# Attention and a gated feed-forward on one core: the order of all queues searched anew, with a port lock in the plan and products on zeros at the start

## The chip, the cores and the metric

One core of a Trainium2 chip runs the whole program in one launch. The metric is device microseconds of one execution; below, TensorE is called PE, VectorE DVE, ScalarE ACT, GpSimd POOL, and SyncE, which issues every DMA, SP, as in the profile.

## The reference

Inputs q, k, v are (8 batches, 8 heads, 576 positions, 64), float32. Everything downstream of `attn_out` is a token-shifted feed-forward with a squared ReLU and a sigmoid gate.

```python
# attention: a coarse one on means of 4 positions, plus a local one (|i - j| < 4)
q_d, k_d, v_d = (x.reshape(B, H, S // 4, 4, D).mean(axis=3) for x in (q, k, v))
out_up = np.repeat(softmax(q_d @ k_d.T / 8) @ v_d, 4, axis=2)
out_local = softmax(where(|i - j| < 4, q @ k.T / 8, -1e9)) @ v
x = (out_up + out_local).transpose(0, 2, 1, 3).reshape(B, S, 512)
# feed-forward
x_prev = x shifted by one position (zeros first)
xk = mu_k * x + (1 - mu_k) * x_prev ;  xr = mu_r * x + (1 - mu_r) * x_prev
out = sigmoid(xr @ w_r) * (maximum(xk @ w_k, 0) ** 2 @ w_v)
```

The weights w_k (512 x 1024), w_v (1024 x 512) and w_r (512 x 512) arrive as 64-bit floats.

## The kernel before

**Tiling.** The attention goes by 32 steps n = 0..31, each a pair of heads of one batch (four steps make a batch). A step turns q and k (`flip` on PE and `turn_part` for the first five, a DVE transpose after that), sums them by fours (`pool_q`, `pool_k`, `pool_v`), makes the scores on PE (`score_both`, later `run_pe`, which also holds the value products of the step before), and goes through two softmaxes: the coarse one (`down_top`, `down_exp`, `down_sum`, `down_norm`, `down_turn`, `down_copy`) and the local one (`score_top`, `score_sub`, `score_exp`, `score_sum`, `score_norm`, `score_turn`, `spread`). `av_pe` multiplies with v; `av_up`, `av_two`, `av_out` put the sum into the tile `xt` of the batch. All scores of a step lie in one PSUM tile, of which there is one.

The feed-forward goes by ten chunks c of 512 or 256 positions. The mix of a chunk is `mix_prev` (x_prev scaled), `mix_part` (mu times x added), `mix_high` and `mix_low`, the two halves into which a float32 is split for products in the faster number format. For chunk 0 the mix xk is made on PE instead (`mix_pe` with diagonal matrices, then `mix_split`, `mix_rest`). Then come eight `k_pe` (12 products of 512 columns each), `k_relu`, `k_high` (square and high half), `k_low`, the gates (`r_pe`, `gate`), 16 `v_pe`, `store_mul` and `store_out`.

Each of the 20 weight blocks of 512 KB is fetched and turned from 64-bit to two halves: `weight_scale` (ACT), `weight_shift` and `weight_tail` (DVE), `weight_high` (ACT), and the low half by `weight_diff` on PE with `weight_left` on ACT (blocks 0 to 7, those of w_k) or by `weight_low` on POOL.

**Order.** The class `Plan` holds every step as a task with its engine, its time and its tiles. `arrange` goes through the tasks in the order that the string `ORDER` spells (two characters a task), gives each a start by its model, chooses PSUM banks, and the program is emitted in that order; so each engine's queue is fixed by the string, and every engine works its queue in order. `fill` then puts products on the matrix `nidn` (`keep_warm`, line 482) where the model sees PE idle in the first 100 us. An SP task in those 100 us also waits until the DMAs before it, but for the last 5.2 us of modelled transfer, have landed (`landed_before`, line 1268).

## Time and profile before

| | us |
|---|---|
| runs | 645.09 median of 3 (644.08, 645.09, 646.65) |
| span of the profiled execution, first to last instruction | 644.7 |
| PE busy | 628.7 (98%) |
| DVE, ACT, POOL busy | 423.2 (66%), 426.4 (66%), 310.4 (48%) |
| DMA, mean over the span | 112 GB/s |
| first `k_pe` begins at | 68.24 |
| last run of products (12 of L972) | 637.55 to 640.46 |

The span is the profiled execution's own time; no other figure for that execution is given, and it lies 0.4 us under the median. Matmuls overlap their neighbours, so a busy PE need not be one at its best; the stretch before the first `k_pe`, called the prologue here, is where PE works in many small steps.

### The profile page before, as it was taken

To read this page: it belongs to the slowest core of one execution; us is meant where nothing else is said; L and a number is where in the kernel's file an instruction comes from. 1 tells how busy PE (TensorE), PEld (TensorE's weight loads), DVE (VectorE), ACT (ScalarE), POOL (GpSimd) and SP (SyncE) were. 2 spreads that over 40 slices of the span, in tenths; PEclk is the share of its full clock that TensorE was granted. 3 is DMA by queue.
4 is the path that set the end of the run, shared out by engine and by line. 5 is a ranking of instruction groups with operands and counts; after the bars stand their busy time and mean duration, and the time that the engine had idled before them with its cause. 6 is when DMAs were issued, how large, how long until landed. Compare 5 with 4: busy or idle time off the path is not lost.

```text
span 644.7 us, 17973 instructions
## 1 busy us (share of the span) xinstructions
PE 628.7 (98%) x6984; PEld 517.5 (80%) x6984; DVE 423.2 (66%) x796; ACT 426.4 (66%) x993; POOL 310.4 (48%) x465
## 2 busy tenths in 40 slices
PE   6989999999999999999999999999999999999997
PEld 6666788878888887888888888888888788888886
DVE  3885966598578876874489856697578744612312
ACT  4886966666767857784859775677667847634442
POOL 5686799855762657334454546345763440000000
PEclk9997999999999999999999999999999999999999
DMA  8888987635566464615655546546574320100001
GB/s 266 282 228 164 230 134 132 132 63 121 116 142 120 107 135 86 137 29 121 138 130 119 107 95 125 101 92 137 111 147 104 86 59 0 50 17 0 25 11 65
DMA packets 251574, 71.90 MB, mean 112 GB/s; under 512 B 224346, under 2 KB 243170, under 8 KB 251490
## 3 DMA queue, kind: packets, MB, share of 16 engines
q1 hardware_dynamic: 251490, 70.76, 49.6%
q8 instruction: 55, 0.90, 0.6%
q14 instruction: 29, 0.24, 0.1%
HBM read 56.85 MB, written 13.86 MB: 110 GB/s over the span
## 4 chain that ended last, share of the span: by engine, by line
PE 83%; DMA 5%; DVE 5%; POOL 2%; SPq 2%; ACT 1%; issue 1%; DVEq 0%; POOLq 0%; ACTq 0%
PE ps_g L940 29%; PE acc L988 28%; PE ps_r L972 12%; PE ps_v L796 6%; PE ps_a L646 3%; DMA wk<-in_moe_w_k_dram 2%; DVE mix L910 2%; DMA kraw<-in_k_dram 2%; PE ps_a L709 1%; PE ps_m L918 1%; PE ps_f L552 1%; DMA wv<-in_moe_w_v_dram 1%; PE ps_a L651 1%; DVE xks L932 1%; DMA qraw<-in_q_dram 1%
## 5 line engine op out<-in xcount | busy, mean ns | idle before, releaser
L940 PE MATMUL ps_g<-xks,wk 128*128 128x512 f32 (+1 forms) x960 | 207.0, 370 | 1.8 <-DVE xks L932 1.0
L940 PEld LDWEIGHTS ps_g<-xks,wk 128*128 128x128 f32 x960 | 168.0, 189 | 33.9 <-DVE xks L932 1.3
L988 PE MATMUL acc<-wv,kh 128*128 128x512 f32 x578 | 180.4, 393 | 0.0
L988 PEld LDWEIGHTS acc<-wv,kh 128*128 128x128 f32 x578 | 106.3, 188 | 22.1
L988 PE MATMUL acc<-wv,kl 128*128 128x512 f32 x289 | 112.6, 390 | 0.0
L972 PE MATMUL ps_r<-wr,xr 128*128 128x512 f32 x432 | 104.0, 392 | 0.1
L972 PEld LDWEIGHTS ps_r<-wr,xr 128*128 128x128 f32 x432 | 80.5, 188 | 17.5 <-DVE xr L932 0.5
L910 DVE SCALAR_TENSOR_TENSOR mix<-xt,mus,mix 128x256 f32<-128x256 f32 (+3 forms) x184 | 88.5, 527 | 7.6 <-ACT mix L905 7.4
L960 DVE TENSOR_TENSOR kl<-kk,kh 128x512 fp32r<-128x512 f32 (+1 forms) x63 | 45.5, 723 | 68.2 <-ACT kh L953 68.0
L742 POOL TENSOR_TENSOR an<-ad,sd 64x144 f32<-64x144 f32 (+2 forms) x128 | 66.7, 531 | 31.9 <-DVE sd L733 24.6
L947 ACT ACTIVATE kk<-ps_g 128x512 f32<-128x512 f32 (+1 forms) x80 | 43.3, 548 | 55.6 <-PE ps_g L940 51.6
L905 ACT ACTIVATE mix<-xt,mus 128x256 f32<-128x256 f32 (+3 forms) x184 | 71.1, 441 | 3.6 <-DVE xr L932 2.2
L674 POOL TENSOR_TENSOR sm<-sm,mx 128x384 f32<-128x384 f32 x28 | 23.9, 853 | 96.5 <-DVE mx L669 96.4
L960 POOL TENSOR_TENSOR kl<-kk,kh 128x512 fp32r<-128x512 f32 (+1 forms) x17 | 21.2, 1251 | 92.7 <-ACT kh L953 52.5
L988 PEld LDWEIGHTS acc<-wv,kl 128*128 128x128 f32 x289 | 54.3, 188 | 11.8 <-DVE kl L960 0.4
L953 ACT ACTIVATE kh<-kk 128x512 fp32r<-128x512 f32 (+1 forms) x80 | 47.2, 589 | 17.1 <-PE acc L988 15.0
L796 PE MATMUL ps_v<-bd,vw 64*64 64x48 f32 x1536 | 52.2, 219 | 1.1 <-issue 1.1
L796 PEld LDWEIGHTS ps_v<-bd,vw 64*64 64x64 f32 x1536 | 48.0, 136 | 1.3 <-issue 1.3
L610 POOL TENSOR_TENSOR tk<-kz 64x288 f32<-64x288 f32 (+1 forms) x56 | 39.8, 711 | 18.6 <-DVE kz L590 7.4
L952 ACT ACTIVATE kk<-kk 128x512 f32<-128x512 f32 (+1 forms) x80 | 46.5, 581 | 0.8
L688 POOL TENSOR_TENSOR sm<-sm,ssum 128x384 f32<-128x384 f32 x32 | 29.2, 913 | 28.8 <-DVE ssum L684 17.1
L864 ACT ACTIVATE up<-ps_v 128x144 f32<-128x144 f32 x32 | 9.3, 290 | 50.0 <-PE ps_v L796 25.7
(108 smaller groups left out, 984.3 us busy)
## 6 DMA issues: line engine op xcount, KB each, us to landing
vw<-in_v_dram SPq DMA_DIRECT2D x126, 96.0 KB, 2.9
out_dram<-sig SPq DMA_DIRECT2D x35, 256.0 KB, 2.3
v<-in_v_dram SPq DMA_DIRECT2D x32, 256.0 KB, 3.6
qraw<-in_q_dram SPq DMA_DIRECT2D x108, 72.0 KB, 2.5
kraw<-in_k_dram SPq DMA_DIRECT2D x108, 72.0 KB, 2.5
wk<-in_moe_w_k_dram SPq DMA_DIRECT2D x8, 512.0 KB, 5.7
wv<-in_moe_w_v_dram SPq DMA_DIRECT2D x8, 512.0 KB, 6.2
keys<-blocks SPq DMA_DIRECT2D x96, 40.0 KB, 1.8
```

Source lines behind the costliest of these rows:

```text
L610: nc.gpsimd.tensor_tensor(out=tk[h], in0=k4[:, :, 0:2], in1=k4[:, :, 2:4], op=ALU.add)
L742: nc.gpsimd.tensor_tensor(out=x, in0=y, in1=z, op=ALU.mult)
L796: nc.tensor.matmul(pv[r][64 * e:64 * e + 64, cols], lhs, rhs, start=(i == 1), stop=(i == NG + 1 + (r != e)))
L905: nc.scalar.activation(mixes[c, h, nm][:, p, o:o + L], xts[b][:, p, s:s + L], AF.Copy, scale=rest)
L910: nc.vector.scalar_tensor_tensor(out=to[:, p, o:o + L], in0=xts[b][:, p, s + 1:s + 1 + L], scalar=mu[:, p:p + 1], in1=to[:, p, o:o + L], o ...
L940: nc.tensor.matmul(ps, w_k_part(p, f, w), x[:, :, y, p, :], start=(m == 0), stop=(m == len(mm) - 1))
L947: nc.scalar.activation(kk, kq[c, f].rearrange("p h t -> p (h t)"), AF.Relu)
L952: nc.scalar.activation(kk, kk, AF.Square)
L953: nc.scalar.activation(kh, kk, AF.Copy)
L960: eng.tensor_tensor(out=kl, in0=kk, in1=kh.bitcast(F32), op=ALU.subtract)
L972: nc.tensor.matmul(ps, x[:, y, p, o:o + P], ws[f"r{p}"][:, w, :], start=(m == 0), stop=(m == len(mm) - 1))
L988: nc.tensor.matmul(accs[c, t][:, j], x[:, o:o + P], ws[f"v{f}"][:, w, j], start=(f == 0 and m == 0), stop=(f == NF - 1 and m == 2), skip_g ...
```

## The change

It replaces the model in `Plan.arrange`, the string `ORDER`, and the engine of 239 of the 1992 tasks, and changes a few steps at the start:

- The model takes DVE and POOL as holders of one exclusive port lock for the operations in `LOCKED` (each part of an operation waits until the other engine's part has ended), and a clock for PE that depends on its recent work.
- A string table `ELSE` moves tasks to another engine. Read out, it moves, from ACT to DVE: 57 `mix_prev`, 19 `mix_high`, 13 `av_up`, 9 `spread`, 5 `weight_high`, 3 `down_copy`; from POOL to DVE: 20 `score_norm`, 13 `pool_k`, 9 `pool_q`, 9 `pool_v`, 9 `score_sub`, 9 `k_low`, 3 `down_norm`, 1 `weight_low`; from POOL to ACT: 22 `down_norm`; from DVE to POOL: 27 `k_low`; and 11 `turn_part` change between ACT and DVE.
- `fill` and its `keep_warm` products go (`FILLERS = ()`). In their place `clear_warm` (DVE) clears 128 columns, and `warm` lets PE multiply them nine times, before the first `flip`.
- `load_consts` is split into `load_identity` and `load_band`; the first DMA is now q of step 0.
- `clear_edge` clears the edge of a window of v on POOL, in tasks of their own, not on DVE inside `load_windows`.
- The diagonals use the buffer of `xr`, not one of the two of `f32tmp`.
- Steps named in `HEADS`, `BITS`, `WPSUM`, `MIXPS` exist in the code, but those lists are empty, so nothing of them is emitted.

The strings read out, from the start to the last window of v that the prologue needs (SP), and to the first `k_pe` (PE; wd is `weight_diff`, sb `score_both`, dt `down_turn`; the 37 steps are the same ones, and `warm` is new). w is a fetch of a weight block, q and k a `load_raw`, v4 and win the two loads of v:

```
SP before  consts q0 k0 w4 q1 w3 w1 k1 q2 w0 w2 w10 mus k2 w5 v4.0 q3 w8 w13 k3 q4 w7 v4.1 w19 k4
           win0 w6 w16 v4.2 win1 w11 win2 v4.3 win3
SP after   q0 ident k0 q1 w1 band w3 w5 k1 q2 w0 mus w7 k2 w4 w13 v4.1 q3 k3 v4.0 w2 q4 w6 k4
           w8 win0 w10 win1 win2 v4.3 v4.2 win3
PE before  flip0q flip0k flip1q sb0 flip1k flip2q wd3 sb1 mus flip2k wd1 wd4 flip3q wd0 wd2 dt0 sb2 wd5
           flip3k wd7 flip4k flip4q av0 dt1 sb3 mix0 wd6 av1 dt2 sb4 av2 dt3 mix1 av3 mix2 mix3 dt4 k_pe
PE after   warm flip0q flip0k sb0 flip1q wd1 flip1k wd3 flip2q flip2k sb1 wd5 wd4 wd0 mus flip3q sb2 dt0
           flip3k wd7 flip4k flip4q wd2 sb3 av0 dt1 wd6 av1 dt2 sb4 mix0 av2 dt3 mix1 av3 mix2 dt4 mix3 k_pe
```

Before the first `k_pe`, the queue of DVE holds `weight_shift` and `weight_tail` for 14 blocks before the change and for 11 after it.

```diff
-KLPOOL, KLF = 1, (3,)
-FLIPACT = (("q", 1), ("k", 0))
+HEADS = ()
+FILLERS = ()
+WARM = 9
 ORDER = """
...
+ELSE = dict(
+    ACT="""
...
-    SHARED = "weight_low k_low mix_low mix_part pool_v".split()
+    LOCKED = dict(
+        DVE=("weight_low k_low mix_low mix_part mix0_low mix0_part pool_v pool_q pool_k score_sub score_norm down_norm "
+             "weight_high mix_high mix0_high mix_prev mix0_prev spread weight_bits").split(),
+        POOL="weight_low k_low pool_v pool_q pool_k score_sub score_norm down_norm diagonals double_mask weight_bits".split())
...
+        def part_of(eng, now, us):
+            got, others = now + self.ENTER, pair[other[eng]]
+            while any(x <= got < y for x, y in others):
+                got = next(y for x, y in others if x <= got < y)
+            e = got - self.ENTER + us
...
+    def clear_warm():
+        nc.vector.memset(xks[:, 0, 0, 0, 0:P].bitcast(F32), 0.0)
+
+    def warm(bank):
+        ps = pp.tile([P, 512], F32, tag=plan.bank[bank], name="ps_x", bufs=1)
+        x = xks[:, 0, 0, 0, 0:P]
+        for _ in range(WARM):
+            nc.tensor.matmul(ps.rearrange("p (a c) -> p a c", a=4), x, x[:, None, :].broadcast_to([P, 4, P]), start=True, stop=True)
+
+    def clear_edge(n):
+        st.setdefault(n, {})["vw"] = vw = wp.tile([P, 12, D], F32, tag="vw", name="vw", bufs=3)
+        if n == 0:
+            nc.gpsimd.memset(vw[0:32, 0, :], 0.0)
+        else:
+            nc.gpsimd.memset(vw[96:128, 11, :], 0.0)
...
+    def engine():
+        return {"DVE": nc.vector, "POOL": nc.gpsimd}[now["eng"]]
+
+    def copied(out, x, **scale):
+        if now["eng"] == "ACT":
+            nc.scalar.activation(out, x, AF.Copy, **scale)
+        elif scale:
+            nc.vector.tensor_scalar(out=out, in0=x, scalar1=scale["scale"], scalar2=None, op0=ALU.mult)
+        else:
+            engine().tensor_copy(out=out, in_=x)
...
-            nc.scalar.activation(mixes[c, h, nm][:, p, o:o + L], xts[b][:, p, s:s + L], AF.Copy, scale=rest)
+            copied(mixes[c, h, nm][:, p, o:o + L], xts[b][:, p, s:s + L], scale=rest)
...
-        nc.scalar.activation(mixed(c, h, nm)[:, 0], mixes[c, h, nm], AF.Copy)
+        copied(mixed(c, h, nm)[:, 0], mixes[c, h, nm])
...
-    emitted = plan.fill(plan.arrange(), keep_warm)
...
+    for t in plan.arrange():
+        now["eng"] = t["eng"]
```

## Rows read from the trace of the kernel before

**Rows 1.** The page: instructions' busy time by engine over the span.

```profile
PE 628.7 (98%) x6984; PEld 517.5 (80%) x6984; DVE 423.2 (66%) x796; ACT 426.4 (66%) x993; POOL 310.4 (48%) x465
```

**Rows 2.** Busy time by stretch; last three columns: granted clock, DMA share, GB/s.

```profile
5.86:11.23 5.37, 5.37 (x101) 5.37 (x102) 1.58 (x3) 2.66 (x5) 2.07 (x10) 1.00 0.98 367
11.23:36.10 24.87, 23.97 (x564) 17.53 (x561) 20.93 (x41) 20.01 (x50) 15.56 (x27) 1.00 0.87 279
36.10:55.60 19.50, 16.54 (x501) 13.39 (x501) 15.06 (x33) 15.09 (x43) 17.07 (x28) 1.00 0.89 202
55.60:62.40 6.80, 6.80 (x52) 4.26 (x55) 2.83 (x7) 3.80 (x14) 3.83 (x7) 0.50 0.77 143
62.40:68.24 5.84, 5.72 (x53) 3.23 (x47) 4.38 (x10) 4.75 (x12) 3.05 (x5) 1.00 1.21 230
68.24:560.00 491.76, 489.86 (x5332) 405.45 (x5333) 355.95 (x668) 343.10 (x800) 261.42 (x378) 1.00 0.52 108
560.00:640.44 80.44, 80.44 (x403) 68.27 (x401) 21.74 (x37) 34.82 (x69) 2.03 (x2) 1.00 0.07 26
```

**Rows 3.** Timeline of the first 38 us, SP and PE: start, us, engine, line, what.

```profile
0.73 0.68 SPq L389 DMA_DIRECT2D mask<-in_band_dram  x1
...
5.86 2.19 PE L552 MATMUL ps_f<-small,qraw 64*64 64x64 f32 x36 [5.86 <-DMA qraw<-in_q_dram]
...
9.73 1.92 PE L552 MATMUL ps_f<-small,qraw 64*64 64x64 f32 x36
...
13.92 1.26 PE L552 MATMUL ps_f<-idn,kraw 64*64 64x64 f32 x36
...
37.29 1.27 PE L552 MATMUL ps_f<-idn,kraw 64*64 64x64 f32 x36 [1.16 <-DMA kraw<-in_k_dram]
```

**Rows 4.** Timeline of PE between 45 and 71 us.

```profile
45.20 1.99 PE L918 MATMUL ps_m<-xt,diag 128*128 128x512 f32 x4
...
54.37 0.29 PE L796 MATMUL ps_v<-bd,vw 64*64 64x48 f32 x4 [1.07 <-issue]
...
57.41 3.76 PE L918 MATMUL ps_m<-xt,diag 128*128 128x512 f32 x4
...
68.24 3.01 PE L940 MATMUL ps_g<-xks,wk 128*128 128x512 f32 x12
```

**Rows 5.** The chain that ended last, in order of time: start, us, what.

```profile
2.13 3.59 DMA qraw<-in_q_dram
...
10.37 6.09 DMA wk<-in_moe_w_k_dram
...
32.44 4.72 DMA kraw<-in_k_dram
...
67.49 0.70 DVE xks L925
```

**Rows 6.** Waits of PE over the span: who for whom, total, times, longest.

```profile
PE ps_g L940 <- DVE xks L932: 1.0, 1, 1.0
```

**Rows 7.** Timeline of DVE and of POOL from 70.5 us.

```profile
70.95 2.67 DVE L910 SCALAR_TENSOR_TENSOR mix<-xt,mus,mix 128x256 f32<-128x256 f32 x3
...
71.84 1.50 POOL L491 TENSOR_TENSOR wr<-w,wr 128x512 fp32r<-128x512 f32 x1 [0.31 <-ACT wr L469]
```

**Rows 8.** Groups of DVE and of POOL by form: busy, mean ns, idle before.

```profile
L910 DVE SCALAR_TENSOR_TENSOR mix<-xt,mus,mix 128x256 f32<-128x256 f32 x88 | 51.7, 612 | 6.1 <-ACT mix L905 6.0
L960 DVE TENSOR_TENSOR kl<-kk,kh 128x512 fp32r<-128x512 f32 x49 | 37.9, 776 | 53.6 <-ACT kh L953 53.4
...
L932 DVE TENSOR_TENSOR xks<-mix,xks 128x1024 fp32r<-128x1024 f32 x16 | 20.4, 1275 | 9.8 <-ACT xks L928 9.8
...
L668 DVE TENSOR_TENSOR sm<-ps_a,mask 128x384 f32<-128x384 f32 x28 | 15.3, 548 | 7.9 <-PE ps_a L709 6.9 <-ACT ad L726 0.9
...
L610 POOL TENSOR_TENSOR tk<-kz 64x288 f32<-64x288 f32 x48 | 34.4, 717 | 15.5 <-DVE kz L590 7.4 <-DMA keys<-blocks 6.2
...
L674 POOL TENSOR_TENSOR sm<-sm,mx 128x384 f32<-128x384 f32 x28 | 23.9, 853 | 96.5 <-DVE mx L669 96.4
```

More of the change, by code (lines that the diff above doesn't have):

```diff
@@ new lines, in parts, with close, advance @@
+    def parts(self, eng, us):
+        parts = self.PARTS.get((eng, us), (us,))
+        return parts, (us - sum(parts)) / max(1, len(parts) - 1)
+    def arrange(self):
+        tasks, ids = self.tasks, decoded(ORDER)
+        assert sorted(ids) == list(range(len(tasks)))
+        end, free, held, taken = {}, {}, {}, {}
+        banks, self.bank, self.when, self.after = [None] * self.BANKS, {}, {}, {}
+        dma_free, table = 0.0, 1
+        pair, begun, other = dict(DVE=[], POOL=[]), {}, dict(DVE="POOL", POOL="DVE")
+        tick, done, warm, sent = self.PHASE - self.TICK, 0.0, False, []
+        def part_of(eng, now, us):
[3 more added lines that the diff above has]
+            e = got - self.ENTER + us
+            late = max((e - x for x, _ in others if got < x < e), default=0.0)
+            free[other[eng]] = free.get(other[eng], 0.0) + late
+            pair[eng].append((got, e))
+            del pair[eng][:-self.KEPT]
+            return e
+        def close(eng, i, e):
+            begun.pop(eng, None)
+            end[i], free[eng] = e, e - self.TAIL[eng]
+            if tasks[i]["lock"]:
+                held[tasks[i]["lock"]] = e
+            self.when[i] = (self.when[i][0], e, e)
+        def advance(eng, t=1e12):
+            while eng in begun and begun[eng][-1] <= t:
+                i, parts, gap, k, now = begun[eng]
+                e = part_of(eng, now, parts[k])
+                if k == len(parts) - 1:
+                    close(eng, i, e)
+                else:
+                    begun[eng] = (i, parts, gap, k + 1, e + gap)
@@ L283, in over @@
         def over(tile):
+            for eng in ("DVE", "POOL"):
+                if eng in begun and begun[eng][0] in self.tile_users[tile]:
+                    advance(eng)
             return max((end[u] for u in self.tile_users[tile]), default=-1.0)
@@ L288, in arrange @@
             eng = t["eng"]
+            for x in ("DVE", "POOL"):
+                if x in begun and (x == eng or begun[x][0] in t["deps"] or t["lock"] and tasks[begun[x][0]]["lock"] == t["lock"]):
+                    advance(x)
             sync = self.WAIT[eng]
@@ L293, in arrange @@
             for d in t["deps"]:
-                s = max(s, end[d] + (self.SAME if tasks[d]["eng"] == eng and not tasks[d]["dma"] else sync))
+                same = tasks[d]["eng"] == eng and not tasks[d]["dma"]
+                s = max(s, end[d] + (self.SAME if same else sync) - self.lead(t, tasks[d]))
             for tile, tag in t["new"]:
@@ L1083, in value_steps @@
     def value_steps(n):
-        R1 = after(n)
         b, p = divmod(n, NP)
-        add("ACT", 0.29, R1 + 1, av_up, n, r=[f"pv{n}"], new=[(f"up{n}", "up")])
-        add("DVE", 0.3, R1 + 2, av_two, n, r=[f"pv{n}b"], w=[f"up{n}"])
+        add("ACT", 0.296, av_up, n, r=[f"pv{n}"], new=[(f"up{n}", "up")], alt=dict(ACT=0.296, DVE=0.3))
+        add("DVE", 0.289, av_two, n, r=[f"pv{n}b"], w=[f"up{n}"])
         if p == 0:
-            add("POOL", 0.1, R1, new_x, b, new=[(f"xt{b}", "xt")], w=[(f"xt{b}", i) for i in range(NP)])
@@ L1210, in attention_moe, with parts_of @@
-    begin_all()
-    add("ACT", 0.3, -60, turn_sign, r=["idn"], w=["nidn"])
-    add("ACT", 0.3, -105, scale_identity, r=["idn"], w=["small"])
-    add("POOL", 0.4, -60, double_mask, r=["mask2"], w=["mask3"])
+            add("ACT", 1.055, mix_high, c, h, nm, r=ps, new=[(to, nm)], alt=dict(ACT=1.055, DVE=0.694))
+            add("DVE", 1.226, mix_low, c, h, nm, r=ps, w=[to])
+    def parts_of(nm, c, h, ps=range(NP)):
+        if c == 0 and nm == "xk":
+            return [f"{nm}0.{h}"] + [(f"{nm}0.{h}", p, *y) for y in ((), (1,)) for p in ps]
+        return [f"{nm}{c}.{h}"]
@@ L1214, in attention_moe @@
+    add("ACT", 0.255, copy_mus, r=["mus"], w=["mu"])
+    if MIXPE:
+        add("POOL", 1.93, diagonals, "xk", r=["mu", "idn"], new=[("diagxk", "xr")])
+    add("ACT", 0.306, turn_sign, r=["idn"], w=["nidn"])
+    add("ACT", 0.306, scale_identity, r=["idn"], w=["small"])
+    add("POOL", 0.42, double_mask, r=["mask2"], w=["mask3"])
     for i in range(len(WORDER)):
```

736 lines of the change are left out of this document (345 added, 391 removed).

## The prediction

> **What bounds the kernel now.** I read the page first: PE is busy 98% of the span, the other engines at most 66% [rows 1]. So time can only come from stretches in which PE waits, or works at its lower clock. The second view was therefore busy time by stretch, cut where PE's work changes [rows 2]. From the first `k_pe` at 68.24 to the last product PE waits 572.2 - 570.3 = 1.9 us in all: 1.9 in the part up to 560 us, nothing behind it. The longest single wait there is 1.0 us, for the low half of chunk 1's mix on DVE [rows 6]. Hence no order of the queues gains more than about 2 us behind 68.24, and whatever else there is to gain lies in the prologue, or in what comes before and after PE's work.
>
> The prologue runs from 5.86 to 68.24, 62.38 us. Three losses can be read in it.
>
> First, the clock at the start. No clock is recorded for the first stretch, so its 1.00 tells nothing [rows 2], but the instructions do: the three `flip`s up to 11.23 take 2.19 to 1.92 us, the same 36 products later 1.26 [rows 3]. That is 1.2 against 2.4 GHz. Three at a mean of 2.06 instead of 1.26 cost 2.4 us. PE had worked for 5.37 us when it ended.
>
> Second, the clock falls again: 55.60 to 62.40 has a granted clock of 0.50, the 1.2 GHz level [rows 2], and a `mix_pe` there takes 3.76 us instead of 1.99 [rows 4]. In 19.5 us before it PE was busy 16.54, and the order of PE in the front part shows what with: between wd6 and mix1 only small products of av, dt and sb. At the full clock these 6.8 us would be 3.4, so 3.4 us are lost.
>
> Third, plain waiting: 62.38 less the five busy times (58.40) is 4.0 us [rows 2], of which 1.2 is the wait for k of step 4 [rows 3] and 1.1 a pause inside an `av_pe` [rows 4]. Together 9.8 us. The chain that ended last tells who sets these waits: from 2.13 to 37.29 it runs through transfers, weight blocks among them [rows 5], and the DMA share is 0.87 to 0.98 in these stretches [rows 2]; behind that it runs through PE itself, and at the end through DVE's `mix_rest` at 67.49 [rows 5].
>
> **The change, part by part.** PE's 37 steps ahead of the first `k_pe` are the same ones, so the sum is made of the losses.
>
> The nine products. SP, the first to work, begins at 0.73 [rows 3]; with DVE's short clearing behind that I put PE's first product at 1.4, an estimate. Twelve such products take 3.01 at the full clock [rows 4], so nine at half of it some 4.5, to 5.9: `flip` 0 begins where it does now, although its q, now the first DMA instead of the fourth, could land at 0.73 + 3.59 = 4.3 [rows 3, 5]. If the clock rises 5.37 us after the first product, as now, it does so at 6.8, and 0.9 us of flips are slow instead of 5.4. About 0.45 of the 2.4 us stay lost: a gain of 2.0. Bounds: nothing, if products on zeros raise no clock, and 2.7, if the clock rises with the last of them and q is taken 0.3 us sooner.
>
> The second fall. mix0, two pairs of 512-column passes, moves from in front of wd6 to between sb4 and av2. The run of small products between two 512-column steps, now av1 to dt3, becomes av1 to sb4, and then av2 with dt3. That breaks the stretch in which the clock fell about in half. I take the whole 3.4 us; bounds 0 and 3.4.
>
> The waits. Ahead of k of step 4, SP now issues nine weight blocks, not eleven. Two blocks of 0.52 MB at 279 GB/s [rows 2] are 3.8 us. PE will come 2.0 us sooner and has waited 1.2, so 3.2 are needed: this wait goes. One block more is left out up to the last window, which lands some 5.6 us sooner. DVE loses three blocks' shift and tail, but gains a `pool_k`, a `pool_v`, two `score_norm` and others of the moved steps: by my count 3 us more, on 44.8 busy of 62.4 us now [rows 2]. With a prologue of 55 us that is 87%, full but not over. ACT loses about 5 us of its 46.3 [rows 2]. I take half of the 4.0 us, 2.0; bounds 0 and 4.0.
>
> The rest at nothing. The three `keep_warm` products go; they stood where PE waited, one of them ahead of the first `k_pe`, which waits for DVE's 67.49 anyway [rows 4, 5]; without such cover each is 0.25 us. `clear_edge` moves two memsets of one row group from DVE to POOL, hidden by POOL's idle half [rows 1]. `load_consts` in two parts adds no DMA. The diagonals' new buffer frees one of `f32tmp` for the mix of chunk 0, and lets `xr` wait for the last `mix_pe` instead; the gates of chunk 0 come far behind.
>
> The moves between engines lie almost all behind 68.24, where PE waits 1.9 us. What they do to DVE: 57 `mix_prev` at 0.45 (the trace has no such copy on DVE; by the mix's own 0.612 [rows 8] as the top and half of it as the bottom, since one source is read and not two) make 26 us, 17 to 35. Nineteen `mix_high` of 1024 columns, by the 1.275 of `mix_low` [rows 8] as the top and half of it as the bottom, at 0.9: 17. Twenty-nine `score_norm` and `score_sub` at 0.548: 16. Pooling and `down_norm`, 35 tasks of some 84 instructions, by POOL's 0.717 and the ratio 0.548 to 0.853 at which an equal shape runs on the two [rows 8]: 39. `spread`, `av_up` and the smaller ones: about 14. Eighteen `k_low` fewer at 0.776 [rows 8]: 14 off. In sum 98 us more on DVE, 423 to about 520, and POOL falls from 310 to about 210. Up to 560 us DVE would be busy 356 + 95 = 451 of 492 us, 92% instead of 72% [rows 2]. POOL and ACT get room. I take it at nothing for PE, since a shorter wait for POOL's slower copies stands against a fuller DVE; bounds 1.9 us gained and some 11 us lost (below).
>
> What the two engines do to each other is in the trace: three `mix_part`s that would take 1.8 at their mean [rows 8] took 2.67, while a subtraction on POOL ran for 1.50 [rows 7]. The Trainium skill (SBUF — State Buffer, section "SBUF: two separate sides") has it that the two share a port pair under an exclusive lock, the loser blocking for the other's whole instruction, while ACT has its own port; the trace agrees that such stretches exist. By that rule this change brings to the lock 76 copies that ran on ACT outside it; with POOL busy a third of the time and 0.67 us an instruction, an estimate of 0.11 us each, 8 us of DVE, no term of the sum, but it speaks for the fourth rival.
>
> **The sum.** 2.0 + 3.4 + 2.0 = 7.4 us: the first `k_pe` at 60.8 and a span of 644.7 - 7.4 = 637.3. The profiled execution lies 0.4 us under the median of the runs shown, so **637.7 us**.
>
> **The rivals.**
>
> (1) The clock falls again, elsewhere in the sparse part: 0.50 for about 6.8 us, 3.4 us back, 641.1. For it: 0.85 busy in the stretch before the fall [rows 2] is no more than the new prologue will have where it waits for transfers. Against: mix0's new place.
>
> (2) The zeros do not raise the clock and the waits stay: the flips cost 2.4 again, only the 3.4 us are gained, 641.7. No product on zeros is in the trace, so nothing excludes it.
>
> (3) DVE in the prologue, at 87%, delays `mix_rest`, as its last one does now [rows 5], and a few chunk starts wait: 4 us of the 7.4 go, or all of it and a little more: 641.7 to 645.5.
>
> (4) Slower: DVE becomes the bound behind 68.24. If its 92% grow by 0.14 us, half of what the three `mix_part`s lost each in their 2.67 us [rows 7], for some 250 operations newly there or newly locked, DVE works 486 of 492 us; today it idles 136 of them, and if a tenth of that, waits for ACT's results [rows 8], cannot be filled, its queue is 500 us long or more, and further delays fall on PE at chunk starts, as the 1.0 us does now [rows 6]. It decides once such stalls exceed 7.4 + 3.2 = 10.6 us, 1.2 us at each of nine chunk starts; I price it at 12 us, 649.5.
>
> **How the numbers follow.** Forecast 0.50; (1) 0.20; (2) 0.09; (3) 0.10; (4) 0.11. About 0.5%, 3.2 us, is what a measurement here tells from no change: faster is below 641.9, slower above 648.3. Faster: all but 0.02 of the forecast, 0.18 of (1), 0.05 of (2), 0.01 of (3), 0.72. Slower: (4) and 0.02 of ill luck besides, 0.13. Same: 0.15. The range goes from 634.3, where all 9.8 us and some of the 1.9 are gained, to 645.5, the end of (3); it leaves out (4) and a little at the low end.
>
> **What would show it.** Right: the first `flip`s at about 1.3 us from 7 us on; no stretch at 0.50 between 40 and 65 us; the first `k_pe` at 60 to 62; k of step 4 landed before PE asks; behind it PE waiting under 2 us in total although DVE is above 85% up to 560 us. Wrong: flips of 2 us behind 8 us; a `mix_pe` of 3.8; PE's waits naming DVE at every chunk's first `k_pe`; or a first `k_pe` on time and the end not, which would put the loss into the moves.

## The result, and the profile after

The changed kernel takes **651.85 us** (median of 4 runs, 650.40 to 653.18), the kernel before in the same job 644.59 us (644.04 to 646.65): a ratio of **1.0114, interval 1.0088 to 1.0141**. It is 1.1% slower; 637.7 was forecast. The profiled execution of the changed kernel took 651.7 us with a span of 649.9.

Busy time by stretch comes first again, cut where PE's work or clock changes: the nine products; the first steps; a fall of the clock; the rest of the prologue; and two stretches behind the first `k_pe`, which begins at 66.03 (cut here at 66.07) where it began at 68.24 [rows 2].

```profile
0.00:5.19 5.19, 4.14 (x10) 2.84 (x10) 0.17 (x1) 1.79 (x3) 4.66 (x14) 1.00 0.60 182
5.19:16.49 11.30, 6.96 (x222) 6.23 (x222) 6.37 (x12) 4.69 (x8) 2.38 (x11) 1.00 0.88 295
16.49:19.91 3.42, 3.42 (x33) 1.95 (x33) 0.41 (x2) 1.51 (x7) 0.00 (x0) 0.50 0.81 236
19.91:66.07 46.16, 43.87 (x1002) 31.64 (x998) 40.09 (x85) 36.11 (x101) 31.19 (x48) 1.00 0.84 204
66.07:560.00 493.93, 489.45 (x5310) 399.98 (x5310) 409.36 (x879) 337.16 (x797) 155.04 (x200) 1.00 0.52 111
560.00:645.70 85.70, 85.66 (x426) 72.50 (x424) 27.17 (x48) 29.26 (x60) 10.10 (x10) 1.00 0.07 25
```

Two things stand in it. The prologue is 2.2 us shorter than that of the profiled execution of before, not 7.4: there is no fall at 55 to 62 us any more, but one at 16.49, half as long, and PE waits (11.30 - 6.96) + (46.16 - 43.87) = 6.6 us between 5.19 and 66.07, where it waited 4.0 [rows 2]. And behind the first `k_pe` the work takes longer. To see that without the cut at 560, one stretch from the first `k_pe` to the last product, for the kernel before and for the changed one:

```profile
68.24:640.45 572.21, 570.31 (x5733) 473.71 (x5733) 377.69 (x704) 377.92 (x868) 263.45 (x380) 1.00 0.46 97
```

```profile
66.03:645.65 579.62, 575.14 (x5734) 472.52 (x5733) 436.57 (x926) 366.41 (x856) 165.14 (x210) 1.00 0.45 98
```

The same products take **579.6 us in place of 572.2, 7.4 us more**. This stretch is the measure of most experiments below. It repeats to 0.1 us with the same prologue (572.20 in another execution of the kernel before, e9). Chunk 0 depends on the prologue in front: the back of the kernel before takes 572.2 to 575.6 us in before, e9, e4, e10, e12, e17 and e18, of which chunk 0 is 73.1 to 75.8 and the rest 499.1 to 499.8 in all seven; the rest of the changed kernel takes 506.0 (505.5 in e3). So differences of 2 or 3 us are safe only behind chunk 0, where the loss is 6.9 us.

Of the 7.4, 2.6 are waits (579.62 - 575.14 against 1.90). The other 4.8 stand as "busy": a product of 512 columns usually adds 0.23 us to PE's busy time, the first behind a wait up to 0.50; 55 of them add over 0.24 us in place of 37, in sum 4.0 us more. DVE is busy 436.6 of 579.6 us, 75%; up to 560 us it is 409.36 of 493.93, 83%, where 92% was forecast.

Who PE and its weight loads wait for behind 66 us (who for whom, total, times, longest):

```profile
PE acc L1033 <- DVE kl L1008: 1.2, 2, 0.7
PE acc L1033 <- ACT sig L1022: 1.0, 2, 0.6
PE ps_r L1017 <- DVE sig L1043: 0.6, 1, 0.6
PE ps_g L982 <- DVE xt L883: 0.5, 2, 0.4
PE ps_g L982 <- DVE xks L970: 0.5, 1, 0.5
...
PEld acc L1033 <- DVE kl L1008: 2.2, 3, 1.1
...
PEld ps_r L1017 <- DVE sig L1043: 1.3, 2, 1.0
```

In before there were two, 1.0 us for DVE's mix [rows 6] and this one for a bank that its `store_mul` still read:

```profile
PE ps_g L940 <- DVE sig L998: 0.6, 1, 0.6
```

Now it is `v_pe` for DVE's `k_low` and for ACT's gate, `r_pe` for DVE's `store_mul`, `k_pe` for a bank that its `av_out` still reads, at most 0.7 us each time. So PE waits mostly for an engine that is idle a quarter of the time. DVE's own longest waits, between 66 and 560 us:

```profile
DVE sm L669 <- PE ps_a L710: 32.0, 19, 6.5
DVE kl L1008 <- ACT kh L1002: 9.7, 8, 3.1
```

It stands at the head of its queue, 19 times, for scores that PE has not computed yet. The longest case, on DVE's timeline (start, us, what, and in brackets the idle time before and what ended it), with the ACT and PE rows beside it:

```profile
294.61 0.67 DVE L771 STREAM_TRANSPOSE blocks<-an 128x480 f32<-128x480 f32 x1
301.82 0.56 DVE L669 TENSOR_TENSOR sm<-ps_a,mask 128x384 f32<-128x384 f32 x1 [6.54 <-PE ps_a L710]
...
302.88 0.77 DVE L577 STREAM_TRANSPOSE qT<-qraw 128x576 f32<-128x576 f32 x1
303.57 0.85 DVE L1008 TENSOR_TENSOR kl<-kk,kh 128x512 fp32r<-128x512 f32 x1
```

```profile
299.66 0.63 ACT L1002 ACTIVATE kh<-kk 128x512 fp32r<-128x512 f32 x1
```

```profile
303.21 0.61 PE L1033 MATMUL acc<-wv,kh 128*128 128x512 f32 x2
304.48 0.50 PE L1033 MATMUL acc<-wv,kl 128*128 128x512 f32 x1 [0.66 <-DVE kl L1008]
```

The inputs of that `k_low` were there at 300.29, when `k_high` ended on ACT, and DVE was idle. But `score_top` and a transpose stood ahead of it in the queue, so it began at 303.57, and PE waited 0.66 us for it.

Last, groups of DVE by form (busy, mean ns, idle before), against [rows 8]:

```profile
L917 DVE SCALAR_TENSOR_TENSOR mix<-xt,mus,mix 128x256 f32<-128x256 f32 x88 | 43.5, 510 | 8.7 <-ACT mix L421 8.4
L1008 DVE TENSOR_TENSOR kl<-kk,kh 128x512 fp32r<-128x512 f32 x36 | 24.9, 695 | 26.1 <-ACT kh L1002 26.1
...
L423 DVE TENSOR_SCALAR mix<-xt,mus 128x256 f32<-128x256 f32 x44 | 16.3, 383 | 0.2
...
L425 DVE CAST xr<-mix 128x1024 fp32r<-128x1024 f32 x10 | 6.9, 691 | 2.5 <-PE ps_r L1017 2.2
```

The moved copies are cheaper than I took them (383 and 691 ns, not 450 and 900), and the operations that were on DVE already got faster, not slower: `mix_part` 510 ns in place of 612, `k_low` 695 in place of 776, now that POOL works 165 us beside them and not 263. For `mix_part` the trace shows it one by one: in before, 46 of the 88 run while an instruction of POOL runs and take 737 ns on average, the 42 others 476; in the changed kernel it is 18 (646 ns) and 70 (475).

### The profile page after: what moved, and what is told of

Read it like the earlier page. It is cut to its first block, busy times and chain, and to the rows that moved or that the text cites. A ratio compares the mean times of both kernels' runs of the same rounds, so it can differ in the third digit from the quotient of the medians.

```text
span 649.9 us, 17978 instructions
## 1 busy us (share of the span) xinstructions
PE 633.5 (97%) x6990; PEld 515.1 (79%) x6990; DVE 484.3 (75%) x1025; ACT 411.1 (63%) x974; POOL 203.4 (31%) x282
## 4 chain that ended last, share of the span: by engine, by line
PE 70%; DVE 8%; DMA 4%; SPq 3%; ACT 2%; issue 1%; POOL 0%; DVEq 0%; POOLq 0%
PE acc L1033 25%; PE ps_g L982 24%; PE ps_r L1017 13%; PE ps_v L803 4%; PE ps_a L647 2%; SPq L513 1%; DMA v<-in_v_dram 1%; PE ps_a L710 1%; DVE sig L1043 1%; DVE kz L591 1%; DMA qraw<-in_q_dram 1%; SPq L778 1%; DMA vw<-in_v_dram 1%; DVE kl L1008 1%; DVE xr L970 1%
## 5 line engine op out<-in xcount | busy, mean ns | idle before, releaser
L1008 POOL TENSOR_TENSOR kl<-kk,kh 128x512 fp32r<-128x512 f32 (+1 forms) x35 | 42.1, 1206 | 162.5 <-ACT kh L1002 134.8
L917 DVE SCALAR_TENSOR_TENSOR mix<-xt,mus,mix 128x256 f32<-128x256 f32 (+3 forms) x184 | 70.7, 424 | 9.1 <-ACT mix L421 8.7
L1008 DVE TENSOR_TENSOR kl<-kk,kh 128x512 fp32r<-128x512 f32 (+1 forms) x45 | 28.7, 640 | 39.6 <-ACT kh L1002 38.4
L421 ACT ACTIVATE mix<-xt,mus 128x256 f32<-128x256 f32 (+3 forms) x114 | 43.4, 430 | 9.4 <-DVE xks L970 4.5
L669 DVE TENSOR_TENSOR sm<-ps_a,mask 128x384 f32<-128x384 f32 x28 | 15.5, 554 | 34.0 <-PE ps_a L710 32.0
L803 PE MATMUL ps_v<-adT,vd 64*64 64x144 f32 x384 | 39.3, 296 | 1.0 <-issue 0.9
L1043 DVE TENSOR_TENSOR sig<-acc,sig 128x512 f32<-128x512 f32 (+1 forms) x37 | 24.2, 666 | 21.0 <-ACT sig L1022 16.6
L591 DVE STREAM_TRANSPOSE kz<-kraw 64x576 f32<-64x576 f32 x48 | 36.5, 760 | 0.7
L675 POOL TENSOR_TENSOR sm<-sm,mx 128x384 f32<-128x384 f32 x19 | 16.0, 842 | 66.4 <-DVE mx L670 57.4
```

The source lines that it names most:

```text
L421: nc.scalar.activation(out, x, AF.Copy, **scale)
L591: nc.vector.transpose(kz[h, e, 3:579], raw[h])
L803: nc.tensor.matmul(pv[r][64 * e:64 * e + 64, cols], lhs, rhs, start=(i == 1), stop=(i == NG + 1 + (r != e)))
L917: nc.vector.scalar_tensor_tensor(out=to[:, p, o:o + L], in0=xts[b][:, p, s + 1:s + 1 + L], scalar=mu[:, p:p + 1], in1=to[:, p, o:o + L], o ...
L1008: engine().tensor_tensor(out=kl, in0=kk, in1=kh.bitcast(F32), op=ALU.subtract)
L1043: nc.vector.tensor_tensor(out=gates[c, t][:, j], in0=accs[c, t][:, j], in1=gates[c, t][:, j], op=ALU.mult)
```

## The experiments

The orders are strings of task numbers; the diffs below write them with task names, BEFORE and AFTER being the two orders and their engines. "Behind" is the time from the first `k_pe` to the last product of the profiled execution; DVE's busy time is that of this stretch. Ratios are to the runs of the kernel before beside each.

| run | us, median | ratio to before | first `k_pe` | behind | DVE |
|---|---|---|---|---|---|
| kernel before | 644.59 | 1 | 68.24 | 572.2 | 378 |
| changed kernel | 651.85 | 1.0114 (1.0088 to 1.0141) | 66.03 | 579.6 | 437 |
| e1 new order, old engines | 672.74 | 1.043 (1.040 to 1.046) | 68.61 | 599.0 | 368 |
| e2 new front, old back | 655.27 | 1.016 (1.0128 to 1.0192) | 66.33 | 581.9 | 383 |
| e3 old front, new back | 650.28 | 1.0073 (1.0032 to 1.0115) | 62.86 | 579.6 | 432 |
| e4 start alone | 643.28 | 0.9981 (0.9953 to 1.0008) | 63.80 | 574.0 | 378 |
| e5 old order, new engines | 676.21 | 1.0497 (1.0441 to 1.0553) | 67.82 | 601.2 | 446 |
| e6 copies to DVE alone | 651.66 | 1.0125 (1.0061 to 1.0189) | 64.29 | 581.7 | 409 |
| e7 `k_low` moves alone | 646.66 | 1.0035 (1.0015 to 1.0055) | 63.60 | 575.8 | 367 |
| e8 `score_top` later | 653.91 | 1.015 (1.0107 to 1.0192) | 65.30 | 581.8 | 438 |
| e9 before again | 647.41 (one) | | 69.09 | 572.2 | 378 |
| e10 start without products | 646.44 | 1.0027 (0.9999 to 1.0055) | 67.42 | 573.0 | 379 |
| e11 other moves alone | 662.52 | 1.0283 (1.0239 to 1.0326) | 65.69 | 590.2 | 420 |
| e12 filled pause | 644.25 | 1.0006 (0.9976 to 1.0035) | 62.78 | 572.9 | 379 |
| e13 short copies | 657.33 (one) | | 73.54 | 577.8 | 424 |
| e14 short mixes | 648.61 (one) | | 66.32 | 576.2 | 374 |
| e15 new order, copies on ACT | 662.50 | 1.028 (1.0253 to 1.0308) | 68.84 | 589.6 | 405 |
| e16 new order, `k_low` back | 657.01 | 1.0183 (1.0158 to 1.0207) | 68.88 | 583.9 | 450 |
| e17 mix0 moved | 644.62 | 1.0019 (1.0000 to 1.0038) | 65.03 | 573.1 | 378 |
| e18 two fillers | 643.76 | 0.9980 (0.9954 to 1.0007) | 63.98 | 575.6 | 377 |

**Where the loss is, and whose: order or engines.** e1 gives every moved operation its old engine back; e2 and e3 cross the two prologues with the two backs; e4 changes the start alone.

```diff
-ELSE = dict(ACT="""...""", DVE="""...""", POOL="""...""")
+ELSE = dict()                                                   # e1
...
-ORDER = AFTER
+ORDER = AFTER[:k_pe(0, 0)] + the rest in the order BEFORE       # e2
+ORDER = START[:k_pe(0, 0)] + the rest in the order AFTER        # e3
+ORDER = START                                                   # e4
...
+START = load_raw(0, q), load_identity, load_band, scale_identity, clear_warm, warm, then BEFORE
```

> The new order of all queues, but each of the 239 operations that the change moved between engines runs on its old engine again. Theory A (the moves fill DVE and with it cost the 7.4 us that are lost behind the first k_pe): DVE falls from 484 to some 400 us of busy time, the stretch from the first k_pe to the last product from 579.6 to 572 to 575 us, the time to 644 to 647 us. Theory B (the new order itself has no slack, whichever engine works): that stretch stays at 578 us or grows, the time is 650 us or more.

> The changed kernel's tasks up to the first k_pe, with its engines, and behind them the tasks of the kernel before in their old order on their old engines. Theory A and B both put the 7.4 us into what comes behind the first k_pe: first k_pe at 66, 572 us from there to the last product, a time about 2.2 us under the kernel before, 642.4 us. Rival C (the new prologue hands over something late, such as weight blocks or windows that have not landed, and the back pays for it): the stretch behind takes 575 to 580 us and the time is 645 to 650 us.

> The prologue of the kernel before, with the nine products on zeros and q as the first transfer, and behind the first k_pe the changed kernel's order and engines. Theories A and B: 578 to 580 us behind the first k_pe, and with a first k_pe at 66 to 68 a time of 650 to 654 us. Rival C (the loss is handed over by the new prologue): 572 to 574 us behind it and 643 to 646 us.

> The order and the engines of the kernel before throughout, with only the start changed: q is the first transfer, DVE clears a tile, PE multiplies it nine times, GpSimd clears the edge, and the diagonals have the new buffer; the three products that kept PE busy in waits are gone. The prediction's first term: the first flips take 1.3 us in place of 2.1, the first k_pe comes 2.0 us sooner, at 66.2, the time is 642.6 us; the second fall of the clock (mix_pe of 3.8 us) stays. Rival D (PE only comes sooner to a wait for k, or the clock falls in another place): first k_pe at 68, 644.6 us.

e3 settles the place: with the old prologue the new back takes the same 579.62 us (the equal hundredth is luck: chunk 0 takes 0.5 us more, the rest 0.5 less). The loss belongs to what comes behind the first `k_pe` and is not handed over by the prologue. e2, which takes 581.9, more than even its rival allowed, does not speak against that: its extra time is all in chunk 0 (82.2 us to the next chunk's first `k_pe`, 73.2 in before; a fall of the clock of 10.2 us, 5.1 us lost, lies in it), where the two halves were not made for each other; from chunk 1 on it takes 499.7 us, like e4.

e1 refutes my first theory in its plain form. Taking the moves back does not win the loss back: the stretch grows to 599.0 us (3.4 of them lost at half clock, from 127.10 to 133.93), with DVE at 368, less than in the kernel before:

```profile
68.61:667.66 599.05, 582.65 (x5733) 476.50 (x5733) 368.24 (x709) 388.06 (x881) 260.88 (x381) 0.99 0.45 95
```

e4 is no faster than before beyond its interval, though its first `k_pe` comes at 63.8 (this is taken up below).

**The price of the moves by themselves.** e5 to e7 and e11 keep e4's order and move all operations, or one group.

```diff
-for t in START: engine = that of the kernel before
+for t in START: engine = that of the changed kernel, if t is one of
+    all 239 (e5) | 57 mix_prev, 19 mix_high (e6) | 36 k_low (e7) | the other 127 (e11)
```

> The order of the kernel before with the start of e4_start_alone, and each of the 239 moved operations on its new engine, at the place in the order where it stood. e1 showed that the new order with the old engines takes 599 us behind the first k_pe, so the new order needs the moves; this run tells what the moves cost by themselves. Theory A (a fuller DVE delays PE): DVE at 480 us, 577 us or more behind the first k_pe where e4 took 574, a time of 648 us or more. Theory B (the new order is what costs): 572 to 575 us behind the first k_pe and 641 to 645 us.

> The order and engines of e4_start_alone, with only the 76 mix copies (57 mix_prev, 19 mix_high) moved from ACT to DVE. DVE gets 57 x 0.383 + 19 x 0.69 = 35 us more and ACT is freed of more than that. Theory A: part of the loss, 575 to 577 us behind the first k_pe. Theory B, or the wait for ACT's copies that goes: 571 to 574 us and 640 to 643.5 us.

> The order and engines of e4_start_alone, with only k_low moved as in the change: 27 from DVE (0.69 us each) to POOL (1.30), 9 from POOL to DVE. If the 0.6 us more of each on POOL reaches v_pe, which reads what k_low writes, the v_pe stall and the stretch behind the first k_pe is 577 to 590 us, the time 646 us or more. If v_pe comes late enough, nothing: 574 us and 643 us.

> e4_start_alone with the moved operations other than the 76 mix copies and the 36 k_low: pooling, score_norm, score_sub, spread, av_up and the weights' high halves to DVE, 22 down_norm from POOL to ACT. All moves together cost 27.3 us behind the first k_pe in the old order (574.0 to 601.2), the copies alone 7.7, k_low alone 1.8. If costs add, these cost 18 us: 592 us behind the first k_pe, 661 us. If instead it is the sum of all that overfills DVE, they cost less alone: 576 to 585 us, 645 to 654 us.

The same stretch of e4, e5, e6, e7 and e11:

```profile
63.80:637.77 573.97, 571.77 (x5735) 473.49 (x5734) 378.38 (x704) 378.45 (x870) 265.44 (x383) 1.00 0.47 98
```

```profile
67.82:669.06 601.24, 580.06 (x5735) 475.29 (x5734) 445.71 (x920) 357.64 (x847) 166.57 (x211) 1.00 0.44 93
```

```profile
64.29:645.98 581.69, 575.43 (x5735) 474.73 (x5734) 409.29 (x793) 337.55 (x783) 264.48 (x383) 1.00 0.45 97
```

```profile
63.60:639.40 575.80, 572.08 (x5735) 473.60 (x5734) 367.37 (x686) 378.63 (x870) 284.18 (x401) 1.00 0.46 98
```

```profile
65.69:655.93 590.24, 578.37 (x5735) 476.21 (x5734) 420.18 (x850) 398.95 (x934) 146.03 (x193) 0.99 0.45 95
```

All moves cost 27.3 us in the old order. The copies alone (31 us of DVE) cost 7.7, the `k_low` 1.8, the others 16.3, in sum 25.8. These prices hold falls of the clock behind the first `k_pe`, which e4 and e7 do not have: 3.4 us at half clock in e5 and in e6, 1.7 lost each, and two such in e11, 3.4 lost. Without them the prices are 25.6 for all, and 6.0, 1.8 and 12.9, in sum 20.7: most of the whole shows with one group at a time, and some 5 us come only when all move. That a fall follows from the waits is not shown. In e6 DVE is busy 409 of 582 us, 70%, and PE still loses some 6 us; the one run of e6 with a mean granted clock of 1.000 took 649.53, 6.2 above the 643.4 of the runs of before at 0.998 or more. e6 lies above the ranges of both its theories, e7 between its two cases, and e11 just under the 592 of prices that add, or between its two cases without its falls. With e1 this makes a square: old order and engines 574.0, new engines alone 601.2, new order alone 599.0, both 579.6. The moves and the order belong together; the new order takes back 21.6 of the 27.3 us that its moves cost, and not the rest.

**Is one group to blame in the new order?** e15 and e16 take one group back in it.

```diff
-ELSE = dict(ACT=..., DVE=..., POOL=...)
+ELSE = the same without mix_prev, mix_high (e15) | without k_low (e16)
```

> The changed kernel's order, with only the 76 mix copies back on ACT. In the old order these copies on DVE cost 7.7 us. If they cost as much in the new order: 572 to 575 us behind the first k_pe and 644 to 647 us. If the new order is built on them (it put other work on ACT in their place): 582 us or more, 654 us or more.

> The changed kernel's order, with only the 36 k_low back on their old engines (27 from POOL to DVE, 9 from DVE to POOL). If k_low on POOL is what holds v_pe up: 575 to 578 us behind the first k_pe and 647 to 650 us. If DVE's time is what is short: 581 us or more, 653 us or more.

No group: copies back, 10.0 us worse; `k_low` back, 4.2 us worse. Both came out as the second of the two cases expected.

**DVE's time, or its place in the queue?** e13 and e14 keep every order, engine and wait of the changed kernel and take working time from DVE (the buffers of the mixes are laid out once at the start, the diagonals in one of them).

```diff
-copied(mixes[c, h, nm][:, p, o:o + L], xts[b][:, p, s:s + L], scale=rest)
+n = min(L, 64) if now["eng"] == "DVE" else L
+copied(mixes[c, h, nm][:, p, o:o + n], xts[b][:, p, s:s + n], scale=rest)
...
-copied(mixed(c, h, nm)[:, 0], mixes[c, h, nm])
+n = 64 if now["eng"] == "DVE" else CT
+copied(mixed(c, h, nm)[:, 0, :, :n], mixes[c, h, nm][:, :, :n])
...
+L = min(L, 64)                     # e14 alone: mix_part, and mix_low in the same way
```

> The changed kernel, its order, engines and waits kept, but each of the 76 copies that moved to DVE writes a quarter of its columns (57 mix_prev 64 of 256, 19 mix_high 256 of 1024); the rest of those buffers holds zeros that DVE writes at the start, so the mixes are not the reference's and the prologue begins some us later. DVE gets about 18 us less work. Theory A (DVE's working time delays PE): 575 to 577 us behind the first k_pe in place of 579.6. Theory B (the places in the queues do): 579 or more.

> As e13_short_copies, and DVE's mix_part and mix_low too work on a quarter of their columns (work left out, the output is not the reference's). DVE gets some 80 to 90 us less work, under 400 in place of 484, less than in the kernel before, with the same queues and waits. Theory A: 572 to 574 us behind the first k_pe. Theory B: 577 us or more.

```profile
66.32:642.55 576.23, 572.96 (x5735) 472.93 (x5733) 374.24 (x926) 366.30 (x856) 161.22 (x211) 1.00 0.46 99
```

Neither theory alone. With 12 us less work on DVE, e13 is 1.9 us shorter; with 62 us less, e14 is 3.4 us shorter, 576.2. DVE's 374 us are then less than the 378 of the kernel before, and 4.0 of the 7.4 us are still there. Behind chunk 0, where the prologue does not mix in, e13 is 1.6 and e14 4.3 us shorter, and 2.7 of the 6.9 us are left. So about half of the loss, or some more, goes with DVE's working time. The rest does not; that it is where things stand in the queues is not shown but for cases like the one above, and PE's longest wait in e14 is 1.1 us for a result of POOL. e8 tried the clearest of these places: in eight of them the next `k_low`, `mix_low`, `mix_high` or `store_mul` goes ahead of `score_top` on DVE, as in

```diff
-DVE: score_top(18), turn_q(20), k_low(3, 4)
+DVE: turn_q(20), k_low(3, 4), score_top(18)
```

> The changed kernel, in whose trace DVE stands 32 us at the head of its queue waiting for PE's scores (score_top, 19 times, up to 6.5 us); in eight places the next k_low, mix_low, mix_high or store_mul now goes ahead of score_top on DVE. Theory H (work that PE needs is held behind score_top): the stretch behind the first k_pe falls from 579.6 to 577 or 578 us. Rival: score_top was itself the urgent one, the stretch stays or grows by 1 to 2 us.

It did what it should where I had looked: DVE's wait for scores fell from 32.0 to 22.9 us, and chunk 3, which holds the case shown above, took 55.7 us in place of 57.1. But chunk 1 took 68.9 in place of 66.5, and the whole 581.8, 2.2 us more. The rival was right in sum, and the likely reason is its own, that elsewhere `score_top` was itself what the next steps waited for. These swaps therefore do not show which places cost the rest.

**The prologue.** e9 is the kernel before once more, e10 is e4 without the nine products, e12 adds ten products that do nothing in front of `score_both` of step 0, e17 moves mix0 on top of that, e18 adds five products in front of `score_both` of step 4 instead.

```diff
-WARM = 9
+WARM = 0                           # e10, with clear_warm and warm left out
...
+FILLERS = (10,)                    # e12, e17: keep_warm(0, 10) in front of score_both(0)
+FILLERS = (10, 5)                  # e18: and keep_warm(1, 5) in front of score_both(4)
...
-mix_pe(0, xk, 0), mix_split, mix_rest behind score_both(3)
+mix_pe(0, xk, 0), mix_split, mix_rest behind score_both(4)       # e17
```

> The kernel before, unchanged, in another execution. The prediction took 3.4 us for the second fall of the clock (0.50 from 55.60 to 62.40) as a loss of every execution. In the 27 runs of before that stood beside e1 to e8, the mean granted clock lies at 0.997 or above in 21, and 6.8 us at half clock would give 0.995. Theory: no 0.50 between 40 and 65 us, a mix_pe of 2.0 us throughout, first k_pe at 64.5 to 65.5. Rival: the fall is there again, first k_pe at 68.

> e4_start_alone without the nine products on zeros and the clearing of their tile; q is still the first transfer. If the products are what raises the clock, the first flips take 2 us again and the first k_pe comes 1 to 2 us later than with them, 65 us, 643.5 to 645 us. It also tells where the pause of 2.8 us at PE's 222nd product comes from (in e4, in the middle of a step, released by nothing that the profile shows; in the changed kernel 2.0 us at its 221st): if it is PE's instructions that come late for a PE that starts early, it is shorter or gone here, and the gain of the products is smaller than 2 us.

> e4_start_alone with ten more products that keep PE busy, in front of score_both of step 0, ahead of the pause of 2.8 us at PE's 222nd product. Theory: PE's instructions land at about 14 us whatever PE does before, so the ten products (2.3 us) cost nothing, the pause shrinks to under 1 us, the clock no longer falls at 15.5 us: first k_pe 1.0 to 1.7 us sooner than in e4 (62.1 to 62.8), 641.5 to 642.5 us. Rival: the pause only comes later by as much, the ten products cost their 2.3 us: first k_pe at 66, 645 us.

> e12_filled_pause (12 runs: 641.7 to 648.55 us, median 644.25; 5 of 12 at a mean granted clock of 1.00, these at 641.7 to 643.6) with mix0 moved between score_both of step 4 and av_pe of step 2, where the changed kernel has it. If the run of small products between two 512-column steps is what lets the clock fall, most runs are at 1.00 now and the median is 641.5 to 642.5 us, under both kernels. If the falls come elsewhere or of themselves, the runs spread as before, 643.5 to 645 us.

> e12_filled_pause with five more products (1.1 us) in front of score_both of step 4, ahead of the second pause inside a step (1.42 us in e12, at PE's 1108th product; 1.07 us inside an av_pe in the kernel before). If that pause too ends at a time of its own, the five cost nothing, break the run of small products, and hold the clock: first k_pe at 62.8, two thirds of the runs or more at a mean granted clock of 0.998, median 641.8 to 642.8. If not, they cost their 1.1 us and the runs spread as those of e12: 644 to 645.5 us.

Two facts decide about these terms. The first is a pause of PE inside a step. The start of the changed kernel, then e4 and e9 from the same views, and e12:

```profile
1.05 4.21 PE L362 MATMUL ps_x<-xks 128*128 128x512 f32 x9 [1.05 <-DVE xks L356]
5.19 1.74 PE L556 MATMUL ps_f<-small,qraw 64*64 64x64 f32 x36
6.76 1.21 PE L556 MATMUL ps_f<-idn,kraw 64*64 64x64 f32 x36
9.10 0.92 PE L642 MATMUL ps_a<-mask,idn 128*128 128x192 f32 x4 [1.12 <-DMA mask<-in_band_dram]
...
12.75 1.02 PE L556 MATMUL ps_f<-small,qraw 64*64 64x64 f32 x28
15.78 0.45 PE L556 MATMUL ps_f<-small,qraw 64*64 64x64 f32 x8 [2.00 <-issue]
```

```profile
10.94 0.46 PE L697 MATMUL ps_a<-kd,qd 64*64 64x144 f32 x5
14.23 0.58 PE L697 MATMUL ps_a<-kd,qd 64*64 64x144 f32 x6 [2.83 <-issue]
```

```profile
13.51 0.24 PE L552 MATMUL ps_f<-idn,kraw 64*64 64x64 f32 x1 [1.13 <-DMA kraw<-in_k_dram]
15.35 2.07 PE L552 MATMUL ps_f<-idn,kraw 64*64 64x64 f32 x34 [1.60 <-issue]
```

```profile
9.68 2.58 PE L470 MATMUL ps_x<-nidn 128*128 128x512 f32 x10
...
13.94 0.72 PE L697 MATMUL ps_a<-kd,qd 64*64 64x144 f32 x12
```

The products do raise the clock: the second `flip` takes 1.21 us at 6.76, where the three took 2.19 to 1.92 [rows 3]. But then PE stops, in the middle of a step and released by nothing that the profile shows, behind product 221 in the changed kernel (9 + 36 + 36 + 4 + 96 + 12 + 28, counted from the rows of the timeline) and behind 222 in e4. Of the twenty traces of this study eighteen stop at that count, in whatever step it falls, for 0.7 to 3.2 us. With the old prologue they go on between 13.7 and 15.4 us, e4, which came at 11.4, at 14.2, and e10, which came at 12.9, at 13.8. In e12 the ten products lie in front of it, and PE, which comes later, does not stop; in e17 and e18, with the same ten, it stops for 0.9 us. So a PE that starts earlier waits longer there: that caps what the nine products can bring.

The second fact is the clock. e9 shows the fall again, 6.8 us from 55.86, and another one of 3.4 us from 14.90, and was as slow as the profiled execution of before (647.4 and 646.5). But of the 90 runs of the kernel before beside these experiments, 53 have a mean granted clock of 0.998 or more, which leaves no room for it (6.8 us at half clock would give 0.995); their median is 643.4 us, that of the 18 under 0.996 is 646.5. The fall is real and costs what the prediction said, some 3 us, but it is not in the median run. The expectation for e9 failed, and its count was off too: 19 of those 27 runs, not 21, lie at 0.997 or above.

Is it mix0's place that holds the clock? e17 has no run of 12 under 0.997 where e12 has three at 0.992, but three against none of twelve is little, and e18, with mix0 at its old place, has none either. The traces speak against the place as the cause: of the eleven with mix0 at its old place only before and e9 have the fall near 56 us, the nine with the new start (e3 to e7, e10 to e12, e18) have none there; and of the nine with the new place, e1, e13 and e16 have a fall ahead of mix0, at 34.94, 51.96 and 36.88.

None of the three gains what was expected of it. e12 has its first `k_pe` at 62.78 as hoped, and yet a median of 644.25. e17's comes at 65.03, which is as much as its clock gains. e18 is at 0.998 or more in 11 of 12 runs, but chunk 0 takes 75.8 us; at 643.76 us, 0.9980 of before, it is the best of all here together with e4, and the interval includes no change.

## Why the prediction was wrong

**The step that failed is "the rest at nothing": the moves between engines, behind 68.24.** The prediction costed them at 0 for PE, with a bound of 11 us, and argued from DVE's busy share. Together with the order made for them they cost 7.4 us, which with a prologue that gained next to nothing is the whole 1.1%. e5 shows what they cost without that order, 27.3 us (25.6 without its fall of the clock), e3 that the 7.4 are the back's own. My estimate of DVE's time was too high (520 us, measured 484): the copies came to 37 us where I took 43, and `mix_part`, whose 88.5 us I left as they were, fell to 70.7. The conclusion from it was too low, because I took DVE's time to cost PE nothing until DVE is full. By e14 about half of the loss goes with DVE's time although DVE is never full; and in the case followed above PE waits because a result that it needs stands behind something else in DVE's queue. In before, PE waited 1.9 us in 572, so there was next to no room for that to get better, and I read this as a reason why the moves could be ignored; it is the reason why they had far more to lose than to gain. "A shorter wait for POOL's slower copies stands against a fuller DVE" weighed two things of which the first had next to nothing to give.

**The second fall, 3.4 us.** The sign came true: it is not in the changed kernel's profiled execution between 40 and 65 us. The mechanism, mix0's place, is not shown, since e3 to e7 lose that fall without it. The size was wrong: the term was taken from one execution and the sum compared to a median in which most executions have no such fall; with a median of 643.4 us where no such fall can be and of 644.3 over all 90, about 1 us of it is in the median of before. And the changed kernel has a fall of its own at 16.49, 3.4 us at half clock, 1.7 us lost; none of its four runs reaches 0.998, and the one at 0.994 has room for more than that.

**The nine products, 2.0 us.** Right in mechanism; in size they bring little. This loss too was read from one execution: in e9, the same kernel, the three flips take 2.19, 1.60 and 1.23 us, which loses half of the 2.4. e4 with them and e10 without: 0.9981 and 1.0027 of before, intervals that touch. By the profiled executions, less their falls (1.7 and 3.4 us), the first `k_pe` is at 62.1 and 64.0, 1.9 us apart as forecast; but the pause eats part of any earlier start, and e4's back takes 1.8 us more than that of before, 1.1 of it in chunk 0.

**The waits, 2.0 us.** Wrong in sign: 6.6 us in place of 4.0. The wait for k of step 4 is gone, as forecast, but others came. The change has the band's load sixth in SP's queue, not first, and PE waits 1.12 us for it; it waits 0.6 for the `pool_k` of step 0 that is now on DVE; and the pause of 2.0 us is new to it (the profiled execution of before has none there, e9 one of 1.6). With two more of its kind, of 0.84 and 0.94 us, these pauses inside steps (the last section takes them up) make 3.8 of the 6.6 us; in before they were 0.44, 0.62 and 1.07. I had counted weight blocks only.

**The time of before.** I put the profiled execution 0.4 us under the median. Each run of the two kernels lies 1.8 to 1.9 us above its span (651.7 and 649.9; in e9 647.4 and 645.6), so the span of 644.7 belongs to a run of about 646.5, as slow as the slowest of those shown. Taken rightly, the same sum would have given 639 us, still far off.

**The rivals.** The fourth, given 0.11, came true in its sign and its place, by stalls that did not need its condition. That its 649.5 lies near 651.9 is luck: it put 12 us behind 68.24 and a prologue 7.4 us shorter, and what was measured is 7.4 us behind and hardly any gain ahead. It wanted DVE at 486 of 492 us through waits for the port; DVE was at 409 of 494, and the operations that share the port with POOL became faster. By the rule of the Trainium skill that I had cited (SBUF — State Buffer, "SBUF: two separate sides"), less POOL work means fewer blocked instructions; the trace agrees, 612 to 510 ns for `mix_part`, and I had looked only at what the moves bring to the lock and not at what they take from it. The first rival, a fall elsewhere, also came, at half its price. The third was right that the prologue's DVE would be needed on time (`pool_k`), at 0.6 us.

**What stays open.** What makes up the 2.7 to 4.0 us that remain with a light DVE was not found; e8 shows one place in the queue that costs and a sum over eight that loses. Nor is it shown why the clock falls where it does. That PE waits for its code (below) is read from times and counts; no run changes the code's transfer.

## What to carry to other kernels

An engine's busy share does not tell whether work can be moved to it for nothing: with every queue in order, 31 us of copies moved to an engine that was 66% busy cost the bound engine 7.7 us, some 6 without a fall of the clock, and PE's longest waits there were for results of that engine; ask of each moved instruction what stands behind it in the new queue and who waits for that. Where the bound engine waits 1.9 us in 572, a new order of everything else can gain 1.9 us there and lose much more. And before a loss seen in one profiled execution becomes a term of the sum, look whether other executions have it: here the granted clock of the later runs told that.

## What the runs showed that I had not expected

**PE waits for its own code.** The pauses inside steps come at equal distances: behind product 221 or 222, then 348 (e6, e10, e12), 475 (e18), 601 and 854 (the changed kernel), 980 (e4, e6) and 1107 or 1108 (e5, e12), multiples of about 126.5 products apart; the 1.07 us inside an `av_pe` of the kernel before [rows 4] is the one behind 1107. The page of the changed kernel lists the transfers of instructions (packets, MB, share of the 16 engines):

```profile
q8 instruction: 55, 0.90, 0.6%
```

55 transfers of 0.90 MB in all, 16.4 KB each, and PE's 6990 products with as many weight loads: 254 instructions for each. The DMA packets of the traces have the times of these transfers, and the pauses follow them: the first pause ends 1.2 to 1.6 us after the end of the first of them in all eighteen traces that have it (in the changed kernel the transfer takes 13.54 to 14.51 and PE goes on at 15.78; in e4 11.82 to 12.84 and 14.23), and the later pauses 1.2 to 1.9 us after the end of the transfer that their count names. In before and e12, which do not stop, PE comes 1.3 us or more after it. So PE waits there for its next instructions. One transfer costs PE 2.0 us in the prologue of the changed kernel, where the DMA share is 0.88 between 5.19 and 16.49 us, and up to 3.2 us in e13. And it may cost twice: in nine of the eighteen the clock falls within 1.4 us of the pause's end, as in the changed kernel at 16.49 and in e4 at 15.49; in the other nine it does not. The Trainium skill (Runtime: NRT & Kernel Launch, "Instruction fetch mechanics") has it that an engine's instructions come in blocks of 16 KiB, 256 instructions, fetched by the sequencer while it works, at a cost that is mostly hidden. The counts agree with the blocks, 254 instructions to a transfer; the cost does not, it is not hidden in this prologue.

**The clock of one program differs between its runs.** The 90 runs of the kernel before, with one and the same program, have mean granted clocks from 0.989 to 1.000, and their time follows: 643.4 us at 0.998 or more, 644.8 at 0.996 to 0.997, 646.5 below. A gain of 0.3% in a prologue cannot be told from that by a few runs.
